# The orders, engine choices and buffer places of a five-engine kernel made anew

## The chip, the cores and the metric

The kernel runs on one core of a Trainium2 chip. A core has TensorE (PE, matrix products), VectorE (DVE), ScalarE (ACT), GpSimd (POOL) and SyncE (SP, which here issues every DMA); each works through its own queue of instructions in order, and a semaphore holds an instruction until what it needs is there. The metric is the device time of one execution in microseconds (us).

## The reference

Attention with random features, and then a feed-forward layer, on 8 batches of 8 heads with 576 rows of 64 elements:

```python
def phi(x):
    proj = np.einsum('bhsd,md->bhsm', x, omega)          # m = 128 features
    sq = np.sum(x * x, axis=-1, keepdims=True) / 2.0
    h = proj - sq
    h = h - np.max(h, axis=-1, keepdims=True)
    return np.exp(h) / np.sqrt(m)
q_p, k_p = phi(q * scale), phi(k * scale)
kv = np.einsum('bhsm,bhsd->bhmd', k_p, v)
z = np.sum(k_p, axis=2)
num = np.einsum('bhsm,bhmd->bhsd', q_p, kv)
den = np.einsum('bhsm,bhm->bhs', q_p, z)[..., None] + 1e-06
x = (num / den).transpose(0, 2, 1, 3).reshape(4608, 512)
h = x @ w_in                                             # 512 x 2048
out = np.maximum(0.01 * h, h) @ w_out                    # 2048 x 512
```

## The kernel before

The 4608 tokens are worked in 9 blocks of 512 (`NB`). For each block there are features of the queries (`query_block`), and for each batch features of the keys and the sums kv (`key_batch`); heads go in pairs `hp` of 0 to 3. Then `feed_forward` runs the block through both weights. Nearly every operand of the products is split into two float16 parts, a high one (a rounded copy, helper `high`, L689, L691 or L693) and a low one (the rest, helper `low_`, L699), and three matmuls take the place of one. The first two key batches and the first query block take an exact float32 way instead (class `Whole`, L1060 the projection, L1068 and L1076 its row maxima, L1078 the subtraction).

The weights have to be made ready in the opening. They come as 64-bit words in 8 pieces each (loads L810 and L812). A piece is put together from its bits on ACT, DVE and POOL (`Weight.convert`: L825 to L855), a column sum finds its scale (L845 on PE), and `Weight.split` makes the two parts (L691 or L693 the high one; L896 on DVE or L699 the low one). `values` finds the largest element of a batch's values (two reductions L1116 on DVE) and scales them (L1139). L733 with L737 to L742 turns a largest element into a power of two.

The names in the text: k*ij* and q*ij* are key batch or query block *i*, head pair *j*; w1*i* and w2*i* are the pieces of the two weights. L1189 and L1201 to L1203 are the sums kv, L1306 to L1308 (L1313 in block 0) the numerators, L1223 the low part of kv, L1283 and L1254 transposes by PE in block 0. L1468 and L1522 are the first layer (L1522 the seven-product form from block 2 on), L1704 the second one, L1629 the second one in the last two blocks. L783 is a warming matmul: it works on whatever lies in the omega tile and its result is not used.

What sets the order is `Plan`. Every step of the program becomes an `Op` with a number, the engines it can run on (`ways`) and the buffers it uses. `forward` is a list scheduler; here its order is thrown away, and `ORDER` gives the sequence in which all steps are written into the five queues, `ON` the engine of those that have a choice. The places of the buffers (which of the `row`, `big` or `ring` tiles a step gets) are still those that `forward` gave. The warming runs are placed by `forward` too (in gaps that it expects on PE before the first product of the feed-forward); `ORDER` names them by numbers past the last step.

```python
        if ORDER:
            by = {o.number: o for o in done}
            assert len(by) == len(ORDER)
            for n, e in ON.items():
                o = by[n]
                o.engine, (o.cost, o.run, o.held) = e, o.ways[e]
            done = [by[n] for n in ORDER]
```

## Time and profile before

| what | value |
|---|---|
| median of 3 runs | 909.47 us (908.52 to 910.31) |
| span of the profiled execution, first to last instruction | 907.4 us |
| median less span | 2.1 us |
| PE busy | 887.9 us, 98% |
| DVE busy | 790.7 us, 87% |
| ACT busy | 536.3 us, 59% |
| POOL busy | 240.5 us, 27% |

The span is what the trace shows from the first to the last instruction. The runs add about 2.1 us to it, the start and the end around the program. Busy time of PE counts the warming matmuls, and it counts a matmul from its start to its modelled end, so that a PE that is shown busy can still do nothing useful. Times in the trace are from the span's start.

### The profile page before, as it was taken

The numbers are of one execution on the slowest core, as the hardware profiler recorded it, in microseconds if no ns is written. First come the engines' busy times: TensorE is split into PE (matmuls) and PEld (weight loads), VectorE is DVE, ScalarE is ACT, GpSimd is POOL, SyncE is SP. The second block draws the span as 40 slices with busy tenths as digits, with TensorE's granted clock in tenths as the row PEclk, the third lists the DMA queues.
The fourth block names the chain that finished last, engine by engine and source line by source line (L and its number), as shares of the span: only waits on it lengthen the run. The fifth ranks groups of instructions, "written<-read, shape, count | busy, mean of one in ns | idle before, by whom it ended". The sixth has DMA issues, their size and how long they took to land.

```text
span 907.4 us, 20572 instructions
## 1 busy us (share of the span) xinstructions
PE 887.9 (98%) x8257; PEld 640.6 (71%) x8257; DVE 790.7 (87%) x1571; ACT 536.3 (59%) x825; POOL 240.5 (27%) x236
## 2 busy tenths in 40 slices
PE   7999989999999999999999999999999999999998
PEld 6888545554556975688568855886579656888887
DVE  7999989978999999999998999899998999952771
ACT  5688877467655774477546854686557533522530
POOL 2332234456341330220211330132001101331340
PEclk9999999999999999999999999999999999999999
DMA  9757456766899979897899897987999636443401
GB/s 353 282 212 220 123 122 139 181 179 138 180 225 230 270 209 208 231 251 178 195 231 225 196 257 167 245 232 157 187 201 252 156 78 215 146 101 115 164 1 47
DMA packets 274879, 170.13 MB, mean 187 GB/s; under 512 B 191072, under 2 KB 237920, under 8 KB 273760
## 3 DMA queue, kind: packets, MB, share of 16 engines
q1 hardware_dynamic: 274784, 168.82, 73.3%
q8 instruction: 64, 1.05, 0.5%
q14 instruction: 31, 0.25, 0.1%
HBM read 105.87 MB, written 16.78 MB: 135 GB/s over the span
## 4 chain that ended last, share of the span: by engine, by line
PE 75%; DVE 12%; DMA 6%; ACT 4%; issue 2%; SPq 1%; POOL 0%; ACTq 0%; DVEq 0%
PE late L1522 14%; PE late L1704 13%; PE ffn L1704 13%; PE ffn L1522 13%; PE pj L976 5%; PE late L1629 5%; PE ffn L1629 3%; PE late L1468 2%; PE ffn L1468 2%; DMA t<-qT 1%; PE mi L1306 1%; DMA nat<-kT 1%; DVE wt L835 1%; PE mi L1308 1%; PE mi L1307 1%
## 5 line engine op out<-in xcount | busy, mean ns | idle before, releaser
L1522 PEld LDWEIGHTS <-w 128*128 128x128 f16 x2352 | 228.0, 98 | 30.4 <-issue 0.5
L1704 PEld LDWEIGHTS <-big 128*128 128x128 f16 x1344 | 127.7, 98 | 138.2
L699 POOL TENSOR_TENSOR big<-row,big 128x512 f16<-128x512 f32 x76 | 92.5, 1222 | 307.1 <-ACT big L693 189.8
L1704 PE MATMUL late<-wt,big 128*128 128x512 f16 x672 | 157.5, 379 | 0.0
L1704 PE MATMUL ffn<-wt,big 128*128 128x512 f16 x672 | 157.0, 379 | 0.0
L1522 PE MATMUL late<-xt,w 128*128 128x256 f16 x864 | 117.9, 273 | 0.0
L1522 PE MATMUL ffn<-xt,w 128*128 128x256 f16 x840 | 114.9, 273 | 0.4 <-DMA xt<-v 0.4
L1007 ACT ACTIVATE p<-p,little 128x1024 f32<-128x1024 f32 (+1 forms) x60 | 61.0, 1016 | 63.0 <-DVE p L1004 52.9
L984 DVE TENSOR_REDUCE st<-pj 128x8 f32<-128x1024 f32 x68 | 73.2, 1077 | 10.6 <-PE pj L976 10.4
L699 DVE TENSOR_TENSOR ph<-p,ph 128x1024 f16<-128x1024 f32 x56 | 69.3, 1238 | 5.4 <-ACT ph L693 4.7
L1004 DVE SCALAR_TENSOR_TENSOR p<-pj,sc,st 128x1024 f32<-128x1024 f32 (+1 forms) x60 | 67.0, 1117 | 0.8
L1468 PEld LDWEIGHTS <-w 128*128 128x128 f16 x384 | 36.6, 98 | 40.3
L693 ACT ACTIVATE big<-row 128x512 f16<-128x512 f32 x92 | 56.3, 622 | 8.5 <-DVE row L1494 7.7
L1545 ACT ACTIVATE row<-row 128x512 f32<-128x512 f32 x71 | 43.7, 625 | 26.6 <-DVE row L1538 25.6
L936 ACT ACTIVATE z<-nat 128x512 f32<-128x512 f32 (+1 forms) x56 | 36.2, 646 | 31.8 <-DMA nat<-qn 16.2
L1522 PE MATMUL late<-w,w 128*128 128x256 f16 x324 | 53.0, 273 | 0.0
L1522 PE MATMUL ffn<-w,w 128*128 128x256 f16 x324 | 53.0, 273 | 0.0
L1468 PE MATMUL ffn<-xt,w 128*128 128x512 f16 x216 | 50.9, 379 | 0.0
L693 ACT ACTIVATE ph<-p 128x1024 f16<-128x1024 f32 x47 | 49.6, 1055 | 0.9
L699 POOL TENSOR_TENSOR v<-xp,v 128x1024 f16<-128x1024 f32 (+1 forms) x10 | 20.5, 2055 | 109.0 <-DVE v L689 49.4
L852 POOL TENSOR_TENSOR wt<-wt,wt 128x1024 f32<-128x1024 f32 x10 | 25.4, 2550 | 69.8 <-ACT wt L850 36.4
L938 DVE TENSOR_REDUCE sq<-z 128x8 f32<-128x512 f32 (+1 forms) x56 | 39.4, 705 | 4.1 <-ACT z L936 3.9
(300 smaller groups left out, 1893.3 us busy)
## 6 DMA issues: line engine op xcount, KB each, us to landing
w<-w1d SPq DMA_DIRECT2D x196, 256.0 KB, 3.8
v<-vn SPq DMA_DIRECT2D x28, 650.0 KB, 5.0
big<-w_in SPq DMA_DIRECT2D x8, 1024.0 KB, 10.3
big<-w_out SPq DMA_DIRECT2D x8, 1024.0 KB, 5.7
nat<-qn SPq DMA_DIRECT2D x32, 256.0 KB, 3.4
out<-row SPq DMA_DIRECT2D x31, 256.0 KB, 3.0
w1d<-wt SPq DMA_DIRECT2D x16, 256.0 KB, 3.4
nat<-kn SPq DMA_DIRECT2D x12, 320.0 KB, 4.7
```

The lines of the kernel that those rows point to most:

```text
L693: ("ACT", act(n, int(pointer)), lambda: nc.scalar.activation(dst(), src(), AF.Copy, scale=1.0 if scale is None else value()), False),
L699: return ways([(e, c, lambda g=g: g.tensor_tensor(dst(), a(), b(), op=ALU.subtract), True) for e, c, g in (("POOL", pool_(n), nc.gpsimd), ...
L938: op("DVE", dve(n), lambda: nc.vector.tensor_reduce(at(self.sq)[:, :2 * nt], square().rearrange("p (g d) -> p g d", d=D), axis=AX.X, op=AL ...
L976: nc.tensor.matmul(at(pj)[:, 512 * h + c * M:512 * h + (c + 1) * M], at(self.t)[:, 2 * (c0 + c) + h, :], om[:, w, :], start=(w == 0), stop ...
L984: op("DVE", dve(n * M), lambda: nc.vector.tensor_reduce(row(0), pv(), axis=AX.X, op=ALU.max), r=[pj], w=[st], prio=prio)
L1004: op("DVE", dve(n * M), lambda: nc.vector.scalar_tensor_tensor(p(), pv(), down(), row(2).rearrange("p (g o) -> p g o", o=1).broadcast_to([ ...
L1007: op("ACT", act(n * M, 1), lambda: nc.scalar.activation(flat(p()), flat(p()), AF.Exp, bias=shift), w=[p32], r=["ones"], prio=prio)
L1468: nc.tensor.matmul(at(ph), wk[wp][:, c:c + P], xt[:, 512 * xp:512 * xp + 512], start=(i == 0), stop=(i == 3 * KT - 1))
L1522: nc.tensor.matmul(pair(bank)[:, f], wt[:, k, wp, f * P:f * P + P], operand(xname, k, xp), start=(first and f == k == i == 0), stop=(k == ...
L1545: op("ACT", act(512), lambda: nc.scalar.activation(at(g), at(src), AF.Prelu, scale=H_DOWN * (TAIL_DOWN if tail else 1.0), alpha=0.01), r=[ ...
L1629: nc.tensor.matmul(pair(bank)[:, t], g()[:, gp, f, t * P:t * P + P], operand(wname, 2 * q + f, wp), start=(first and q == t == f == i == 0 ...
L1704: nc.tensor.matmul(at(po), g_(q)[:, s, gp, t * P:(t + 1) * P], wf[wp], start=(q == s == 0 and gp == wp), stop=(q == s == 3 and gp == 1))
```

## The change

No step of the program is added or taken away, and no dependency between steps changes. Three tables are new. `ORDER` has another sequence. `ON` gives other engines: between before and after, 28 of the 137 warming matmuls go, 25 low parts (L699) move from DVE to POOL, and DVE gets 9 steps net that ACT had (7 high parts or copies, 2 others). `PLACES` is new: it holds the buffer place of every buffer of every kind, in the order in which the buffers are made. A new function `settle` reads it and asserts that no place is handed out while it is in use. A negative number in `ORDER` stands for a run of so many warming matmuls; there are 9 such runs with 109 matmuls, where there were 10 with 137. `backward` and the passes that used it go; they did not run before (`PASSES = 0`).

```diff
-PASSES = 0
-SHIFT_OP = {...
...
+PLACES = {
+    "xt": [0, 1, 2, 3, 0, 1, 2, 3, 0, 5, 4, 1, 3, 2, 0, 1, 5, 3, 4, 1, 2, 0, 5, 1, 3, 2, 4, 0, 1, 3, 5, 2, 0],
+    "v": [0, 0, 0, 0, 0, 0, 0],
...
 ORDER = [
-    2, 16, 1, 0, 27, 62, 144, 151, 17, 7, 3, 43, 9, 4, 28, 165, 18, 5, 6, 146, 145, 22, 19, 152, 3478, 81, 3461, 20,
...
+    2, 0, 16, 1, 27, 43, 151, 3, 144, 7, 17, 4, 5, 22, 18, 28, 23, 6, 81, 44, 19, 62, 9, 24, 165, 20, -13, 33, 152,
...
-        done = self.forward()
-        for _ in range(PASSES):
...
-            done = [by[n] for n in ORDER]
+        if not ORDER:
+            return self.forward()
+        for o in self.ops:
+            o.engine, o.heat = ON.get(o.number, next(iter(o.ways))), False
+            o.cost, o.run, o.held = o.ways[o.engine]
+        done, heaters = [], len(self.ops)
+        for n in ORDER:
+            if n >= 0:
+                done.append(self.ops[n])
+                continue
+            x = Op()
+            x.number, x.engine, x.heat, x.filler, x.held = heaters, "PE", True, True, False
+            x.cost, x.run = -0.1 * n, lambda n=n: self.warm[1](-n)
+            x.ways, x.before, x.bufs = {"PE": (x.cost, x.run, False)}, [self.warm[0]], []
+            heaters += 1
+            done.append(x)
+        assert sorted(o.number for o in done if not o.heat) == list(range(len(self.ops)))
+        self.settle(done)
         return done
...
+                if b.place is None:
+                    b.place = PLACES[b.kind][nth[b]]
+                    assert b.place < self.places[b.kind]
+                    hosts = [(b.kind, b.place), *shared.get((b.kind, b.place), ())]
+                    assert not any(user.get(k) for k in hosts), f"{b.kind} {nth[b]} has a place in use"
+                    user[b.kind, b.place] = b
+                b.left -= 1
+                if not b.left:
+                    user[b.kind, b.place] = None
```

The lines of the kernel move by 48 (L699 is L747 in the changed one, L1116 is L1164, L1223 is L1271, L783 is L831, and so on). In the rows below a name with a number is a tile (`v_0_99` holds the values of batch 1, `pj_129` and `pj_0_133` are the banks of the projections, `mi` a bank of PE, `big` and `row` hold the hidden layer, `kv_100` the sums of batch 1).

On DVE, some 40 us into the program, where the maxima of the fourth key head pair of batch 0 and the value maxima of batch 1 stand. Before:

```order
53 L1116 TENSOR_REDUCE little<-v_0_99 128x1
54 L1068 TENSOR_REDUCE st_113<-pj_0_133 128x2
55 L1116 TENSOR_REDUCE little<-v_0_99 128x1
56 L1330 TENSOR_TENSOR xp_106<-mi_136,r_125 128x256
57 L833 TENSOR_SCALAR wt_72<-wt_70 128x1024
58 L835 SCALAR_TENSOR_TENSOR wt_72<-big_80,wt_72 128x1024
```

The changed kernel at the same place, and then where the value maxima stand now:

```order
54 L1374 TENSOR_SCALAR r_125<-mi_136,little 128x4
55 L1376 RECIPROCAL r_125<-r_125 128x4
56 L883 SCALAR_TENSOR_TENSOR wt_76<-big_82,wt_76 128x1024
57 L913 TENSOR_REDUCE little<-mi_136 128x8
58 L915 TENSOR_REDUCE little<-little 128x1
59 L1124 TENSOR_REDUCE st_112<-pj_129 128x8
```

```order
142 L998 TENSOR_SCALAR sc_121<-sc_121 128x1
143 L883 SCALAR_TENSOR_TENSOR wt_71<-big_79,wt_71 128x1024
144 L1164 TENSOR_REDUCE little<-v_0_99 128x1
145 L1032 TENSOR_REDUCE st_112<-pj_129 128x8
146 L747 TENSOR_TENSOR z_85<-nat_84,z_85 128x8x64
```

The two value maxima of batch 1 moved some 90 rows back, and the maximum of the projection in `pj_129` now stands in row 59, where it stood in row 64.

On DVE, just ahead of the numerators of q10 (they wait for the last part of batch 1's kv, `kv_100`). Before, and then the changed kernel:

```order
217 L994 SCALAR_TENSOR_TENSOR st_114<-st_114,sc_122,sq_118 128x8
218 L995 SCALAR_TENSOR_TENSOR st_114<-sq_118,st_114 128x8
219 L691 TENSOR_SCALAR kv_100<-mi_136 128x4
220 L1223 SCALAR_TENSOR_TENSOR kv_100<-mi_137,kv_100 128x4
221 L699 TENSOR_TENSOR big_80<-row_104,big_80 128x512
222 L1223 SCALAR_TENSOR_TENSOR kv_100<-mi_136,kv_100 128x4
```

```order
208 L1271 SCALAR_TENSOR_TENSOR kv_100<-mi_136,kv_100 128x4
209 L1042 SCALAR_TENSOR_TENSOR st_114<-st_114,sc_122,sq_118 128x8
210 L1043 SCALAR_TENSOR_TENSOR st_114<-sq_118,st_114 128x8
211 L739 TENSOR_SCALAR kv_100<-mi_137 128x4
212 L1271 SCALAR_TENSOR_TENSOR kv_100<-mi_137,kv_100 128x4
213 L747 TENSOR_TENSOR ph_90<-p_0_88,ph_90 128x1024
```

The last part of kv stood in row 222 of DVE's queue and stands in row 212; the low part of `ph_90`, ahead of it before, stands behind it.

On PE, where the projections of the third and fourth query head pairs of block 0 stand. Before, the run of 18 warming matmuls begins in the last two of these rows:

```order
273 L1060 MATMUL pj_129<-xt_108,nat_84 128x128 x2
274 L1060 MATMUL pj_129<-xt_108,p_0_88 128x128 x2
275 L1283 MATMUL ffn_135<-ident,ph_89 128x128 x4
276 L783 LDWEIGHTS om
277 L783 MATMUL mi_137<-om 128x240
```

```order
294 L1108 MATMUL pj_0_133<-xt_108,nat_83 128x128 x2
295 L1108 MATMUL pj_0_133<-xt_108,z_85 128x128 x2
296 L1361 MATMUL mi_137<-kv_100,qp_97 128x65 x4
297 L1108 MATMUL pj_129<-xt_108,xn_107 128x128 x2
298 L1108 MATMUL pj_129<-xt_108,p_0_88 128x128 x2
299 L1108 MATMUL pj_129<-xt_108,xn_107 128x128 x2
```

In the changed kernel the projections of both pairs follow the transposes at once, the fourth in the second bank; before, runs of 18, 5 and 27 warming matmuls stood ahead of the third.

## Rows read from the trace of the kernel before

**Rows 1.** Busy time of each engine in stretches of the opening; columns first.

```profile
core 0: us, PE busy (x) PEld busy (x) DVE busy (x) ACT busy (x) POOL busy (x), PEclk, DMA share, GB/s
23.00:46.00 23.00, 21.58 (x260) 19.99 (x259) 20.88 (x36) 15.30 (x23) 8.04 (x4) 1.00 0.71 283
0.00:73.50 73.50, 63.88 (x772) 58.80 (x773) 64.07 (x111) 53.44 (x74) 20.81 (x14) 1.00 0.76 287
0.00:138.30 138.30, 124.84 (x1209) 96.25 (x1210) 124.39 (x227) 104.01 (x151) 38.29 (x34) 1.00 0.65 215
```

**Rows 2.** The same view, from 139 us to the end.

```profile
139.00:300.00 161.00, 159.69 (x1277) 89.31 (x1271) 148.46 (x297) 102.95 (x149) 75.25 (x82) 1.00 0.80 189
300.00:500.00 200.00, 199.35 (x1991) 144.83 (x1989) 187.54 (x405) 123.41 (x194) 40.50 (x43) 1.00 0.91 221
500.00:780.00 280.00, 280.00 (x2645) 199.42 (x2643) 260.09 (x527) 165.74 (x260) 52.22 (x50) 1.00 0.83 194
780.00:903.40 123.40, 123.33 (x1129) 110.15 (x1126) 68.68 (x117) 39.51 (x73) 34.22 (x28) 1.00 0.31 92
```

**Rows 3.** Timeline of PE: start, length, instruction, idle time before it.

```profile
7.35 0.64 PE L1060 MATMUL pj<-xt,nat 64*128 64x128 f32 x4
7.78 0.64 PE L1060 MATMUL pj<-xt,z 64*128 64x128 f32 x4
9.44 0.39 PE L1060 MATMUL pj<-xt,nat 64*128 64x128 f32 x4
9.67 0.39 PE L1060 MATMUL pj<-xt,z 64*128 64x128 f32 x4
...
73.48 0.61 PE L1254 MATMUL ffn<-ident,xp 128*128 128x128 f32 x4
74.77 1.46 PE L1468 MATMUL ffn<-xt,w 128*128 128x512 f16 x6
...
124.39 1.05 PE L976 MATMUL pj<-om,t 128*128 128x128 f16 x16 [1.39 <-ACT p L1001]
138.29 0.19 PE L1307 MATMUL mi<-kv,qp 128*128 128x65 f16 x1 [0.26 <-DVE kv L1223]
```

**Rows 4.** Groups of instructions, PE: count, busy us, mean ns of one.

```profile
L783 PE MATMUL mi<-om 128*128 128x240 f16 x137 | 15.7, 266 | 0.6 <-DVE xp L1330 0.6
```

**Rows 5.** Timeline of DVE around the two marks.

```profile
45.25 1.22 DVE L1078 TENSOR_TENSOR ph<-pj,st 128x1024 f32<-128x1024 f32 x1
46.39 0.68 DVE L833 TENSOR_SCALAR wt<-wt 128x1024 uint32<-128x1024 uint32 x1
73.05 0.42 DVE L1330 TENSOR_TENSOR xp<-mi,r 128x256 f32<-128x256 f32 x1
128.71 3.38 DVE L896 SCALAR_TENSOR_TENSOR wt<-wt,little,wt 128x1024 f16<-128x1024 f32 x2
```

**Rows 6.** Groups of DVE's instructions in the first 139 us, by shape.

```profile
L1116 DVE TENSOR_REDUCE little<-v 128x1 f32<-128x1280 f32 x6 | 8.8, 1474 | 0.4 <-DMA v<-vn 0.4
L896 DVE SCALAR_TENSOR_TENSOR w<-wt,little,w 128x1024 f16<-128x1024 f32 x6 | 7.7, 1278 | 0.0
L1076 DVE TENSOR_REDUCE st<-pj 128x8 f32<-128x1024 f32 x11 | 13.4, 1217 | 0.8 <-PE pj L1060 0.8
L699 DVE TENSOR_TENSOR big<-row,big 128x512 f16<-128x512 f32 x5 | 3.3, 681 | 0.0
L691 DVE TENSOR_SCALAR w<-wt,little 128x1024 f16<-128x1024 f32 x1 | 0.8, 754 | 0.0
L689 DVE CAST big<-row 128x512 f16<-128x512 f32 x2 | 0.8, 419 | 0.0
L938 DVE TENSOR_REDUCE sq<-z 128x8 f32<-128x512 f32 x4 | 2.6, 677 | 0.0
```

**Rows 7.** Groups of POOL's instructions in the first 139 us, and one later piece's timeline.

```profile
L699 POOL TENSOR_TENSOR big<-row,big 128x512 f16<-128x512 f32 x8 | 9.3, 1183 | 25.7 <-ACT big L693 24.8 <-DMA t<-z 0.8
...
129.69 1.32 POOL L699 TENSOR_TENSOR big<-row,big 128x512 f16<-128x512 f32 x1 [8.97 <-ACT big L693]
```

More of the change, by code (lines that the diff above doesn't have):

```diff
@@ L282 @@
[L282 to L284 removed]
+    41: "DVE", 300: "DVE", 340: "DVE", 349: "DVE", 375: "DVE", 415: "DVE", 440: "DVE", 484: "DVE", 509: "DVE",
+    620: "DVE", 632: "DVE", 675: "DVE", 680: "DVE", 685: "DVE", 695: "DVE", 700: "DVE", 710: "DVE", 715: "DVE",
@@ L285 @@
+    3040: "DVE", 3052: "DVE", 3058: "DVE", 3070: "DVE", 3073: "DVE", 3165: "DVE", 3166: "DVE", 3180: "DVE",
+    3195: "DVE", 3203: "DVE", 3216: "DVE", 3223: "DVE", 3228: "DVE", 3237: "DVE", 3240: "DVE", 3244: "DVE",
+    3249: "DVE", 3255: "DVE", 3282: "DVE", 3309: "DVE", 3328: "DVE", 3351: "DVE", 3354: "DVE", 3363: "DVE",
+    3366: "DVE", 3375: "DVE", 3384: "DVE", 3394: "DVE", 3403: "DVE", 3415: "DVE",
 }
@@ L345, in order @@
     def order(self):
-        done = self.forward()
-        for _ in range(PASSES):
-            late = self.backward(done)
-            for o in self.ops:
-                if not o.filler and o.prio > -0.9:
-                    o.prio = -0.5 + 1e-4 * (late[o.number] + SHIFT_OP.get(o.number, 0.0))
-            done = self.forward()
-        if ORDER:
-            by = {o.number: o for o in done}
-            assert len(by) == len(ORDER)
-            for n, e in ON.items():
-                o = by[n]
-                o.engine, (o.cost, o.run, o.held) = e, o.ways[e]
-            done = [by[n] for n in ORDER]
@@ L361, in order @@
-        return done
-    def backward(self, done):
-        held, at_ = {}, {}
-        done = [o for o in done if not o.heat]
+        if not ORDER:
[14 more added lines that the diff above has]
+            done.append(x)
@@ new lines, in order, with settle @@
+        assert sorted(o.number for o in done if not o.heat) == list(range(len(self.ops)))
+        self.settle(done)
+        return done
+    def settle(self, done):
+        shared = {}
+        for k, hosts in self.over.items():
+            for h in hosts:
+                shared.setdefault(k, []).append(h)
+                shared.setdefault(h, []).append(k)
+        user, last, nth = {}, {}, {b: i for bs in self.kinds.values() for i, b in enumerate(bs)}
+        for bs in self.kinds.values():
+            for b in bs:
+                b.place, b.left = None, len(b.ops)
@@ L367, in backward @@
         for o in done:
-            o.needs = {x.number: x for x in o.before}
             for b in o.bufs:
-                if b not in at_:
-                    hosts = [(b.kind, b.place), *self.over.get((b.kind, b.place), ())]
-                    at_[b] = [held[k] for k in hosts if k in held]
-                    held[b.kind, b.place] = b
-                for x in (x for u in at_[b] for x in u.ops):
-                    o.needs[x.number] = x
-            o.needs.pop(o.number, None)
-        left = dict.fromkeys((o.number for o in done), 0)
@@ L378, in backward @@
-        for o in done:
-            for x in o.needs:
-                left[x] += 1
-        last = max(o.end for o in done)
-        until, late = dict.fromkeys(left, last), {}
-        free = dict.fromkeys(("PE", "ACT", "DVE", "POOL", "SP"), last)
-        port = last
-        todo = [o for o in done if not left[o.number]]
-        while todo:
-            cost = lambda o: o.cost - self.LESS[o.engine]
-            def latest(o):
-                r = min(until[o.number] - (o.end - o.start - cost(o)), free[o.engine])
-                return min(r, port) if o.held else r
-            o = max(todo, key=lambda o: (latest(o), o.start))
-            start = latest(o) - cost(o)
-            todo.remove(o)
-            late[o.number] = free[o.engine] = start
-            if o.held:
-                port = start
-            for n, x in o.needs.items():
-                until[n] = min(until[n], start)
-                left[n] -= 1
-                if not left[n]:
-                    todo.append(x)
@@ L403, in backward @@
-        return late
+                if b.place is None:
[7 more added lines that the diff above has]
+                    user[b.kind, b.place] = None
```

48 lines of the change are left out of this document (24 added, 24 removed), and 395 rows, old and new, of tables (ORDER, PLACES).

## The prediction

> **What bounds the kernel now.** I read first how busy each engine is by stretches. From 139 us on, PE is busy in 159.69 of 161 us, 199.35 of 200, 280.00 of 280 and 123.33 of 123.4 [rows 2]: 2.0 us of idle time in 764. Its matmuls follow each other there as fast as anywhere in the trace, so this stretch is PE's own work, and no order shortens it by more than those 2.0 us. What an order can change lies ahead of it. Up to 138.3 us PE is shown busy for 124.84 us, but 15.7 us of the whole trace are warming matmuls [rows 4], nearly all of them there, so PE does nothing useful in about 29 of these 138 us.
>
> What it waits for is DVE. DVE is busy 20.88 us of the 23 between 23 and 46 us, 64.07 of the first 73.5 and 124.39 of the first 138.3 [rows 1]. So between 73.5 and 138.3 us it is busy in 60.3 of 64.8 us. Two places show PE starting where DVE ends. Call them marks. **Mark 1** is the transposition L1254 for q02 at 73.48; the instruction that it needs, L1330, starts at 73.05 and takes 0.42 [rows 3, 5]. **Mark 2** is the numerator L1307 of q10 at 138.29, which waits for DVE's L1223 [rows 3]; behind it PE is full. As long as DVE is the engine that decides, a mark comes as early as the DVE work ahead of it is done, and what counts is that work less the useful PE work that is already behind PE.
>
> **The change, part by part.** At mark 1, the orders say what DVE has ahead of it. Gone are the two maxima of batch 1's values (2 x 1.474), and the high part (0.754) and low part (1.278) of w14, together 4.98 us; the high part goes to ACT and the rest stands later. In come a subtraction L1078 (1.22), a maximum L1076 (1.217), a low part of 1024 elements (near 1.25) and a short scaling (0.3), 3.99 us [rows 5, 6]. DVE is 1.0 us earlier. PE has more behind it there: the first product of the feed-forward (L1468, six matmuls, 1.3 us from 74.77 to the next) and the projection of k13, eight groups of four at 0.23 us from start to start (9.44 to 9.67), 1.8 us [rows 3]; the exchange of two numerators costs nothing. That is 3.1 us, and with DVE's 1.0 a gain of 4.1 us at mark 1.
>
> At mark 2 the difference is larger. Gone from DVE to ACT: two high parts of a weight piece (2 x 0.754), two of the hidden layer (2 x 0.419) and one of kv (about 0.42, from the same row), 2.77 us. Gone to POOL: four low parts of the hidden layer (4 x 0.681), 2.72 us. Moved behind the mark: a row sum of squares (0.677), the low part of a feature tile (1.22, the length of L1078, which has its shape) and the low part of a weight piece (1.278), 3.18 us. Come in: one low part (0.681) and one high part (0.419), 1.10 us [rows 5, 6]; a few instructions of under 0.3 us on either side are left out. The net is 7.6 us. DVE starts an instruction some 0.08 us before the one ahead has ended (45.25 + 1.22 against 46.39 [rows 5]), and eleven fewer of them give back 0.9, so 6.7 us. PE's own work at mark 2 is nearly the same, 0.5 us more behind it. The gain by DVE alone is 7.2 us.
>
> It isn't all realised. On the way from mark 1 to mark 2 PE also waits 1.39 us at 124.39 for ACT's L1001 [rows 3], which the change leaves alone, and DVE stands 4.5 us idle there for others. I take the 1.4 off: **5.8 us**, between the 4.1 of mark 1 and the 7.2 of mark 2, and the end of the program comes earlier by as much, since PE is full from mark 2 on.
>
> The rest is priced at nothing, with what covers it. The 28 warming matmuls fewer (28 x 15.7/137 = 3.2 us [rows 4]) lie in PE's waits, and give nothing of their own: without them PE would stand. They are how the shorter waits show. Five high parts more are ACT's in the opening, where it is busy 104.01 of 138.3 us [rows 1]; if ACT were late instead, 0.6 us each. The loads of batch 1's values go behind the weight's on SP's queue, and what is queued behind them is the feature and weight loads; they are needed only where DVE now takes their maxima, some 90 DVE rows later, which is the cover. After 139 us DVE is busy 148.46 of 161, 187.54 of 200 and 260.09 of 280 us [rows 2]; the other low parts go to POOL there, which makes room, and PE is the bound with or without it. The waits there, 2.0 us, are drawn anew by new places and orders: from -2.0 (all gone) to +4.0 (three times as many). I take 0.
>
> Warming is the one thing that could be missed. Early in the trace four projection matmuls are 0.43 us apart (7.35 to 7.78), and 0.23 from 9.0 us on (9.44 to 9.67) [rows 3]: the pace of 1.2 and of 2.4 GHz, though the granted clock is printed as 1.00 throughout [rows 1]. One more such slow stretch would cost the six groups of the first one 0.2 us each, 1.2 us; it is in the range.
>
> **Sum.** Span 907.4 - 5.8 = 901.6 us. The median of the runs is 2.1 us above the span: 903.7 us.
>
> **The rivals.** (1) *The gain is given back later.* PE gets to its full stretch earlier, but loads of the first layer's weights and the transposed rows must then come earlier too. In the new order the shortest stretch of PE work between the last use of a weight buffer and the next product from the same buffer is 36 matmuls, where it was 54. For it: the waits on DMA are already among those after 139 us. Against it: one buffer in 186, and 2.0 us in 764 is very little. With 6 us of waits instead of 2: 909.5 - 5.8 + 4.0 = 907.7 us.
>
> (2) *It does not do what it says*: the chain to mark 2 goes through loads, ACT and POOL as much as DVE, PE waits for the next of them, and nothing is won: 909.5 us. For it: DVE's 4.5 us idle between the marks are such waits. Against it: DVE busy for 93% of that time, and PE starting within 0.01 us of DVE's end at mark 1.
>
> (3) *Slower: POOL holds DVE up.* While a POOL low part runs, DVE's work from two buffers can stand: two L896 at 128.71 took 3.38 us, against 2 x 1.278, with a POOL low part from 129.69 to 131.01 in them [rows 5 to 7]. So a part that goes to POOL (1.183 us) may cost DVE more than it did on DVE (0.681). Ten such parts stand ahead of mark 2 in the new order, eight before. If each stopped DVE for its whole length, that is 11.8 us, less the 0.8 that is there already, against the 7.2 gained: 3.8 us later, 913.3 us. It decides from about 10 of the 11.8 us on. Against it: the eight of before cost only about 0.8 us of 9.3. The Trainium skill has this as a rule (SBUF — State Buffer, "Who interferes with whom"): the pair of ports that VectorE and GpSimd share is an exclusive lock for a whole instruction. By that rule in full the sum would be this rival's; the trace agrees at the one place above, and not in the other parts of the opening, so the chance is small.
>
> **How the numbers follow.** Forecast 0.68: gains from 4.1 us to 10.0 us (7.2, the 2.0 of later waits, and the 0.8 of the lengthened L896 pair), 899.5 to 905.4 us. Rival 1 0.15, spread from 906 to 909.4. Rival 2 0.10, around 909.5. Rival 3 0.07, above 911.3. 0.2%, about what a measurement of this kernel can tell from no change, is 1.8 us: faster means below 907.7, slower above 911.3. Faster is the forecast and half of rival 1, 0.75; same is the other half and rival 2, 0.18; slower 0.07. The range takes in the forecast and most of rival 1: 899.5 to 908.8 us.
>
> **What would show it.** In the changed trace, DVE's work ahead of q10's first numerators should be some 7 us less, and these should start at about 132 us; warming matmuls should take near 12.5 us, and no wait of PE for DVE should stand where runs of 18 and 27 stood; from there on PE should be full, with about 2 us idle. Wrong would be the forecast if PE's idle time after mark 2 grew to 6 us (rival 1), if mark 2 stood at 138 again behind waits for ACT or DMA (rival 2), or if DVE's parts from two buffers were longer by more than 9 us in sum (rival 3).

## The result: slower, by an opening that gained and a later part that lost

The changed kernel takes 913.56 us (median of 5 runs, 913.1 to 918.13) against 909.47: a ratio of 1.006 [1.0039, 1.0081]. The forecast was 903.7 us with a range of 899.5 to 908.8, so it is wrong in sign. Beside runs of before on two more chips, the same kernel took 923.36 us (1.0163 [1.0146, 1.0181]) and 919.37 us (1.0124 [1.0087, 1.0162]), while before stood at 908.3 and 908.1. Its three traces are called after, again and third below. The profiled execution of after is the slowest of its five, 918.13 us with a span of 916.4, so its trace holds 4.6 us more than the median. Times and ratios leave out one run below (935.3 us, without warming matmuls), which was in a slow state.

The stretches of after, in the columns of [rows 1] and [rows 2] (stretch, its length, busy us and count of PE, PEld, DVE, ACT and POOL, granted clock, DMA share, GB/s):

```profile
0.00:73.50 73.50, 68.22 (x829) 63.43 (x829) 66.06 (x123) 59.48 (x81) 21.75 (x19) 1.00 0.74 279
0.00:138.30 138.30, 133.01 (x1278) 100.31 (x1279) 129.58 (x235) 115.69 (x163) 46.34 (x41) 1.00 0.70 222
139.00:300.00 161.00, 156.48 (x1291) 92.12 (x1290) 140.72 (x289) 98.20 (x150) 83.21 (x83) 0.98 0.84 193
300.00:500.00 200.00, 193.54 (x1868) 138.02 (x1866) 180.81 (x385) 118.96 (x184) 49.28 (x49) 1.00 0.91 213
500.00:780.00 280.00, 272.90 (x2567) 191.56 (x2566) 242.23 (x498) 145.03 (x232) 64.82 (x59) 0.99 0.81 186
780.00:912.40 132.40, 132.35 (x1230) 118.47 (x1227) 81.56 (x150) 48.07 (x88) 36.53 (x30) 1.00 0.34 102
```

Two things have changed places. In the opening PE is busy for 133.01 us where it was 124.84 [rows 1], with fewer warming matmuls in it. From 139 us on, where before had 2.0 us of idle time [rows 2], the four stretches now leave 4.52, 6.46, 7.10 and 0.05: 18.1 us, and DVE is less busy too, 140.72 of 161 us against 148.46. So nobody is full there: the engines wait for each other. PE's waits in after from 139 us on (engine, operation and line <- engine, tile and line waited for: us in all, times, longest):

```profile
PE pj L1024 <- DVE p L1052: 7.8, 5, 3.7
PE late L1570 <- DMA w<-w1d: 5.1, 5, 2.2
PE mi L1354 <- DMA qp<-ph: 3.7, 1, 3.7
```

Lines of the changed kernel are 48 higher than before's: L1024 is before's L976 (the product behind a pair's features), L1570 its L1522, L1354 its L1306. They wait for DVE, for weights and for transposed rows: several causes. But the places are the same ones. Counting PE's products from the start, without the warming matmuls, nine waits stand ahead of the same products in all three traces: the 1219th, 2235th, 3047th, 3341st, 3699th, 4305th, 5613th, 6355th and 6449th. They are 16.1 of after's 18.1 us, and 14.1 of 15.7 and 13.8 of 16.0 in the other two.

**A measure for the rest.** Idle time misses what PE loses at a lower clock or between matmuls. So I took, for every shape and line of matmul, the median distance from its start to the next start between 139 and 900 us, and added these up over all matmuls but the warming ones. The time passed less that sum is PE's *lost time* up to a point; the end is PE's last matmul. It can be held against the spans: at the end it is 20.9 us for before and 29.9 for after, 9.0 apart as the spans are (916.4 and 907.4). Only differences between rows are to be read. The float32 projections of the opening start by turns some 7 and 105 ns after the one ahead, a median does not fit them, and for it all rows are about 20 us too low, so that after's 2.6 us by 139 us is less than its idle time.

| lost by (us) | 139 | 300 | 500 | end | from 139 on |
|---|---|---|---|---|---|
| before | 15.8 | 18.2 | 19.8 | 20.9 | 5.1 |
| after | 2.6 | 10.7 | 19.4 | 29.9 | 27.3 |
| again | 10.0 | 17.1 | 23.3 | 33.6 | 23.6 |
| third | 9.5 | 15.9 | 24.2 | 32.1 | 22.6 |

By 139 us the changed kernel is 13.2, 5.8 and 6.3 us ahead. Behind that it loses 22.2, 18.5 and 17.5 us more than before.

**Two of the places** that all three traces share. The first, around 275 us in after (start, length, instruction; idle time before it in brackets):

```profile
273.80 2.13 POOL L747 TENSOR_TENSOR v<-xp,v 128x1024 f16<-128x1024 f32 x1 [5.24 <-ACT v L741]
273.81 2.15 DVE L1042 SCALAR_TENSOR_TENSOR st<-st,sc,sq 128x8 f32<-128x8 f32 x1
...
277.49 1.28 DVE L1052 SCALAR_TENSOR_TENSOR p<-pj,sc,st 128x1024 f32<-128x1024 f32 x1
...
278.82 1.87 PE L1024 MATMUL pj<-om,t 128*128 128x128 f16 x16 [3.72 <-DVE p L1052]
```

A DVE step of 128x8 that takes 0.22 us elsewhere takes 2.15, about as long as POOL's low part beside it; 1.5 us of small steps stand between it and L1052; and PE waits 3.72 us. The same place costs 4.24 us in again and 3.43 in third. Behind the wait PE runs at half clock (stretches of after):

```profile
274.00:278.00 4.00, 1.10 (x11) 0.83 (x9) 3.86 (x9) 1.19 (x2) 1.93 (x1) 0.96 1.01 331
278.00:284.00 6.00, 5.18 (x55) 4.67 (x55) 3.19 (x4) 3.69 (x6) 0.00 (x0) 0.50 0.99 283
```

The second is SP's queue and PE at 626 to 636 us in after:

```profile
626.00 3.25 SPq L1291 DMA_TRANSPOSE xt<-xn  x1
629.35 3.67 SPq L1291 DMA_TRANSPOSE w<-v  x1
633.07 1.31 SPq L1322 DMA_TRANSPOSE qp<-ph  x1
...
636.25 0.24 PE L1354 MATMUL mi<-kv,qp 128*128 128x65 f16 x1 [3.70 <-DMA qp<-ph]
```

The transpose that PE needs could have gone from 608.86 us on, when ACT had made its source, and stood behind two large ones that held SP for 6.9 us. PE waits 3.70.

### The profile page after: what moved, and what is told of

The parts are those of the page before. It is cut to its first block, busy times and chain, and to the rows that moved or that the text cites. A ratio compares the mean times of both kernels' runs of the same rounds, so it can differ in the third digit from the quotient of the medians.

```text
span 916.4 us, 20491 instructions
## 1 busy us (share of the span) xinstructions
PE 889.0 (97%) x8229; PEld 640.8 (70%) x8229; DVE 776.5 (85%) x1555; ACT 526.2 (57%) x816; POOL 280.9 (31%) x261
## 4 chain that ended last, share of the span: by engine, by line
PE 47%; DVE 6%; DMA 3%; SPq 2%; issue 1%; ACT 1%; POOL 0%; DVEq 0%; POOLq 0%; ACTq 0%
PE late L1570 10%; PE ffn L1752 8%; PE ffn L1570 8%; PE late L1752 8%; PE ffn L1677 5%; PE late L1677 3%; PE pj L1024 3%; DMA w<-w1d 1%; DMA nat<-kn 1%; DVE ph L747 1%; SPq L1291 1%; DVE st L1032 1%; DVE p L1052 1%; PE mi L1354 1%; DVE z L1009 1%
## 5 line engine op out<-in xcount | busy, mean ns | idle before, releaser
L1570 PEld LDWEIGHTS <-w 128*128 128x128 f16 x2352 | 227.9, 98 | 41.3 <-DMA w<-w1d 6.3
L747 POOL TENSOR_TENSOR big<-row,big 128x512 f16<-128x512 f32 x87 | 108.1, 1249 | 277.9 <-ACT big L741 139.1
L1570 PE MATMUL late<-xt,w 128*128 128x256 f16 x942 | 129.5, 274 | 0.7 <-DMA w<-w1d 0.4
L1570 PE MATMUL ffn<-xt,w 128*128 128x256 f16 x762 | 105.1, 273 | 0.0
L747 DVE TENSOR_TENSOR ph<-p,ph 128x1024 f16<-128x1024 f32 x56 | 69.9, 1248 | 2.4 <-ACT ph L741 2.3
L1052 DVE SCALAR_TENSOR_TENSOR p<-pj,sc,st 128x1024 f32<-128x1024 f32 (+1 forms) x60 | 67.0, 1117 | 0.6
L1570 PE MATMUL late<-w,w 128*128 128x256 f16 x342 | 56.0, 273 | 4.7 <-DMA w<-w1d 4.7
L984 ACT ACTIVATE z<-nat 128x512 f32<-128x512 f32 (+1 forms) x56 | 36.0, 644 | 30.6 <-DMA nat<-kn 10.4
L747 POOL TENSOR_TENSOR xn<-xp,xn 128x768 f16<-128x768 f32 (+2 forms) x13 | 23.7, 1824 | 93.9 <-DVE xn L737 44.2
L1570 PE MATMUL ffn<-w,w 128*128 128x256 f16 x306 | 50.1, 273 | 0.8 <-DVE z L1586 0.7
L1516 PE MATMUL ffn<-xt,w 128*128 128x512 f16 x204 | 48.3, 379 | 0.0
L1024 PE MATMUL pj<-om,t 128*128 128x128 f16 x576 | 40.7, 224 | 5.3 <-DVE p L1052 5.3
```

What stands on the lines that cost most here:

```text
L747: return ways([(e, c, lambda g=g: g.tensor_tensor(dst(), a(), b(), op=ALU.subtract), True) for e, c, g in (("POOL", pool_(n), nc.gpsimd), ...
L1024: nc.tensor.matmul(at(pj)[:, 512 * h + c * M:512 * h + (c + 1) * M], at(self.t)[:, 2 * (c0 + c) + h, :], om[:, w, :], start=(w == 0), stop ...
L1052: op("DVE", dve(n * M), lambda: nc.vector.scalar_tensor_tensor(p(), pv(), down(), row(2).rearrange("p (g o) -> p g o", o=1).broadcast_to([ ...
L1516: nc.tensor.matmul(at(ph), wk[wp][:, c:c + P], xt[:, 512 * xp:512 * xp + 512], start=(i == 0), stop=(i == 3 * KT - 1))
L1570: nc.tensor.matmul(pair(bank)[:, f], wt[:, k, wp, f * P:f * P + P], operand(xname, k, xp), start=(first and f == k == i == 0), stop=(k == ...
```

## Experiments: where the loss lies

Two theories first: the changed sequence behind the opening is itself the slower one; or PE, being ahead, cannot keep a lead that the others can't follow, and any sequence would give it back. So the two kernels were cut and joined: the changed one's opening to 200 us with before's sequence and engines from there, the reverse, and a cut at 575 us. The buffer places were given out anew in these joined kernels, longest free first. In the list of step numbers, the beginning of the first against before's, and its seam (629 is the last step in the changed kernel's sequence):

```diff
 ORDER = [
-    2, 16, 1, 0, 27, 62, 144,
+    2, 0, 16, 1, 27, 43, 151,
...
     699, 711, 689, 920, 854, 629, 921, 690, 572, 1197, 1189, 855,
...
```

> The changed kernel's order and engines for every step that it has begun by 200 us of its trace, and then the order and engines of the kernel before from its 213 us on (the two have done the same steps there, but for 3.5 us of DVE work and 4 us of POOL work; the places of the buffers of the second part are given out again, the one longest free first). At 200 us the changed kernel is 12.2 us ahead of the kernel before in PE's work, and it gives back 21 us from there to the end in the profiled execution. Theory 1 (the waits after the opening belong to the places of the new sequence): the second part keeps the 5 us of lost time that it had, and the lead stays: 909.5 - 12.2 = 897.3 us, 896 to 900. Theory 2 (the lead cannot be held, since DVE, busy 90 to 94% between 139 and 430 us, is the next bound and takes it back whatever the sequence): the lead melts in new waits of PE for DVE before 430 us, 906 to 910 us.

> The opposite graft: the kernel before up to its 213 us, then the changed kernel's order and engines from its 200 us on. Theory 1 (the sequence): the changed kernel's second part loses its 17 to 21 us here too (17 by the median of its runs, 21 by its profiled execution): 926 to 931 us, with the stalls before L1024, L1570 and L1354 in the same places of the program. Theory 2 (the lead): PE comes 12 us later and DVE with it is no more behind than it was in the kernel before; the waits that ate the lead (275 to 430 us, some 11 us) are gone and only those after 630 us stay (9 us): 916 to 919 us.

> The changed kernel up to its 575 us, then the order and engines of the kernel before from its 576.5 us on, places given out again. At 575 us the changed kernel's lead is down to 0.3 us; the 9.2 us that it falls behind come between 630 and 725 us, where PE waits for the transposed queries (L1354, 3.9 us), for weights (L1570, 3 to 4 us) and for little else. Theory 1 (the sequence): these 9 us go and nothing else changes, 904.5 (median less 9) to 909 us (kernel before less 0.3). If they are a matter of what the first 575 us left behind (buffers, queues), they stay: 912 to 915 us.

> The changed kernel once more, for a second trace. Theory 1 and 2: the stalls of PE come at the same steps as in the first trace (before L1024 at 275, 428 and 497 us, before L1354 at 632 us, before L1570 at 394 and 716 us); what varies is their length, and whether PE's clock falls after those of over 3 us. 913 to 918 us. If the stalls sit elsewhere, the trace of one execution says little on where the time goes.

| kernel | us | ratio | lost by 139 | 300 | 500 | end | from 139 on |
|---|---|---|---|---|---|---|---|
| changed to 200, then before | 903.8 | 0.9951 [0.9936, 0.9965] | 9.5 | 12.3 | 14.5 | 15.6 | 6.1 |
| before to 200, then changed | 934.03 | 1.0271 [1.0248, 1.0295] | 15.4 | 24.4 | 32.0 | 46.0 | 30.6 |
| changed to 575, then before | 921.02 | 1.0149 [1.0122, 1.0175] | 9.8 | 14.1 | 20.9 | 31.1 | 21.3 |

None of these four runs took the time that a theory gave it. The first joined kernel lies between its two forecasts: its opening lost 9.5 us by 139 us, as again's did, so the lead was 6.3 us and not 12.2. The other two are slower than either theory said, and again took 923.36 us where 913 to 918 was expected, with its waits at the expected steps.

The first settles it all the same. It comes to 139 us 6.3 us ahead of before and ends 5.3 ahead, 4.5 us in the medians (908.33 to 903.8). Its stretches after 139 us are before's again ([rows 2]):

```profile
139.00:300.00 161.00, 159.29 (x1307) 92.01 (x1306) 146.71 (x298) 106.35 (x161) 80.12 (x83) 1.00 0.85 199
300.00:500.00 200.00, 199.14 (x1978) 144.21 (x1976) 188.15 (x399) 124.66 (x193) 40.06 (x42) 1.00 0.93 218
500.00:780.00 280.00, 280.00 (x2637) 198.97 (x2635) 260.15 (x529) 162.60 (x257) 52.03 (x50) 1.00 0.83 196
```

The lead can be kept, and the second kernel, without a lead, loses 30.6 us behind the opening, a part of it at its seam (waits of 1.38 and 2.43 us at 219 and 226): the theory of the lead falls. The loss belongs to the changed sequence behind some 200 us, with its engines. Nor does it need the buffer places of the changed kernel: in the second 821 of 1681 places are others, and six of the nine waits stand ahead of the same products in it (2235, 3341, 3699, 5613, 6355 and 6449). The cut at 575 us says little on what lies behind it, since the seam itself costs most: 21.8 us are lost by 550 and 30.2 by 600.

**Single places.** The next theory: a handful of badly placed steps make the loss. Two kernels mend the named places by moving steps within one queue, one on DVE and one on SP (seven buffer places with it); one puts warming matmuls ahead of the two products that waited, against the lower clock.

```diff
-    1006, 1240, 1241, 1302, 1303, 1141, 1242,
+    1240, 1241, 1242, 1006, 1302, 1303, 1141,
...
-    2239, 2714, 2386,
+    2239, 2714, 2473, 2386,
...
-    1243, 1262,
+    1243, -32, 1262,
```

The first pair, in which steps of the other engines are left out, puts L1052 (1242) ahead of the small steps of another head pair and of a division (1006); two more L1052 and L1009 are moved alike. The second puts q63's transpose (2473) ahead of the large ones; two weight loads are moved alike. The third is the first of two warming runs.

> The changed kernel beside the three runs that follow, which mend it in places. 913 to 923 us: on the chip of its first runs it was 913.6, on the next one 923.4; the difference stood at 125 us already (2.7 against 10.0 us of PE's time lost by then), where low parts on POOL had come 0.1 us ahead of a step of DVE instead of behind it.

> The changed kernel with three steps of DVE put first where PE waits for them, nothing else: the subtraction L1052 of q30 ahead of four small steps and of the division L1403 that lets POOL start a low part (PE waited 3.7 and 4.2 us there, at 279 and 287 us, DVE's step L1042 had taken 2.15 us beside that low part where it takes 0.22); L1052 of q43 ahead of L1009 (which took 2.12 for 0.74 us beside POOL; PE waited 1.7 us at 430); L1052 of q52 ahead of the five steps L785 to L790 (PE waited 0.8 us at 498). Theory 1 (the waits belong to single places of the sequence): all three go, and with the first the fall of PE's clock: 7 to 9 us less than the changed kernel. Rival (PE is ahead of DVE all over, a wait that is taken away comes back at the next step): under 3 us less.

> The changed kernel with three issues of SP put first: the transposes of q63 (ready 25 us earlier, they stood behind two transposes L1291 that took 3.3 and 3.7 us of SP; PE waited 3.7 and 2.5 us at 636 and 641) ahead of those two; one weight load ahead of the two transposes L1291 at 709 us, and one ahead of a transpose at 386 us (PE waited 2.2 and 1.2 us at 719 and 722, 1.8 and 1.2 us at 396 and 401). Theory 1: these three waits go, with the fall of the clock behind the first: 6 to 9 us less than the changed kernel. Rival (SP's queue is full, something else stands back in its place): under 3 us less, with new waits for transposes or weights within 20 us of the old ones.

> The changed kernel with 32 warming matmuls (3.2 us) ahead of the step that PE waits for at 279 us and 22 (2.2 us) ahead of that at 636 us. They fill waits and remove none: what they can give back is what PE's lower clock costs behind the two waits (granted clock 0.5 of full from 278 to 284 us and from 636 to 639.6 us in the first trace). Theory 1 puts 1.1 to 2.5 us on the first fall and 1.3 to 1.5 us on the second (time lost there less the wait itself): 2.5 to 4 us less than the changed kernel. If the falls cost nothing that counts: the same time within 1 us, or more where a warming run is longer than the wait that is left.

Beside third's 919.37 us they took 918.61, 919.43 and 922.56, with 29.5, 31.0 and 33.7 us lost at the end against 32.1. The first two came out as their rivals said; the third is slower, where a gain or no change was expected. Each mended wait goes or shrinks, and others come. PE's waits from 139 us on with DVE's steps moved:

```profile
PE mi L1342 <- DMA qp<-ph: 2.5, 1, 2.5
PE late L1558 <- DMA w<-w1d: 2.0, 3, 1.0
PE pj L1012 <- DVE p L1040: 1.9, 3, 0.7
PE late L1558 <- ACT row L729: 1.7, 1, 1.7
PE late L1558 <- DVE row L725: 1.2, 1, 1.2
PE late L1558 <- DMA xt<-v: 1.2, 1, 1.2
```

and with SP's steps moved (lines here are 12 lower than after's):

```profile
PE pj L1012 <- DVE p L1040: 7.2, 5, 2.6
PE ffn L1558 <- DVE row L1574: 2.8, 1, 2.8
PE late L1740 <- DVE nat L1574: 2.4, 1, 2.4
```

In the first, waits for L1040 (after's L1052) fall from 7.8 to 1.9 us. The product mended first, the 2235th, starts at 281.61 without a wait, and 4 to 12 us further on, from 285 to 293, the 2281st, 2308th and 2329th wait 1.66, 1.19 and 1.21 us for ACT, for a transposed row and for DVE. In the second the wait of 3.70 us for transposed rows is gone, and waits of 2.75 and 2.44 us stand at 400 and 729, ahead of the 3329th product (12 before a mended one) and of the 6543rd (94 behind another). Warming does keep the clock up at both places (its stretches):

```profile
280.00:284.00 4.00, 3.73 (x41) 3.42 (x39) 3.38 (x9) 0.39 (x1) 0.68 (x1) 1.00 1.07 330
636.00:640.00 4.00, 3.30 (x47) 2.74 (x45) 1.99 (x8) 1.46 (x3) 0.00 (x0) 1.00 0.35 66
```

yet it is the slowest of the three: by 725 us it has lost some 2 us more than third. A wait of 2.73 us for weights stands at 721 us, where third's is 1.47; what holds the weights up there isn't shown. So the theory of single places falls in this form: the waits have their places, but when one is mended the next stands within 100 products of it. The six mended places hold the longest waits, and with all six mended (below, on another chip) 4.4 us of the loss are gone, a quarter.

**Engines or sequence.** Is it the choice of engines (`ON`) or the sequence? Each was tried with the other's partner; 249 steps differ in engine: net, 25 go from DVE to POOL and 8 from ACT to DVE.

> The changed kernel's sequence and places with the engines of the kernel before: 249 steps change their engine (44 of DVE's go to POOL by the change and 19 of POOL's to DVE, 97 of ACT's to DVE and 89 of DVE's to ACT; here they all go back). Theory E (the engines: low parts on POOL stand in DVE's way, 21 us of lengthened steps of DVE after 139 us against 14 before): the waits for DVE go, 905 to 912 us. Theory S (the sequence: PE, DVE and SP are each needed by the next one with no time between, whoever does a step): no better than the changed kernel, 915 to 930 us, since DVE gets 14 us of work back.

> The opposite: the kernel before, sequence and places, with the changed kernel's engines. Theory E: the low parts that go to POOL lengthen DVE's steps here too and PE waits for them: 914 to 925 us. Theory S: the kernel before's sequence holds, 907 to 912 us, within 3 us of the kernel before.

The changed sequence on before's engines takes 950.14 us (1.0457), before's sequence on the changed engines 948.05 (1.0443), with 63.4 and 58.9 us lost. Both are 24 us and more worse than either whole kernel, and beyond what either theory gave. This says that sequence and engines are one thing, each made for the other, and tells nothing on which of them is the weak one in the changed kernel.

**POOL's low parts.** The changed kernel has 25 more of them on POOL. In two kernels POOL's writes zeros in their place, so that it reads nothing from SBUF; a third does so with all six places mended, and a fourth mends these alone.

```diff
-        return ways([(e, c, lambda g=g: g.tensor_tensor(dst(), a(), b(), op=ALU.subtract), True)
+        runs = {"POOL": lambda: nc.gpsimd.memset(dst(), 0.0),
+                "DVE": lambda: nc.vector.tensor_tensor(dst(), a(), b(), op=ALU.subtract)}
...
```

> The changed kernel with every low part that POOL works out (L747 on POOL, 145 of them) set to zero by POOL instead, so that it reads nothing and is done sooner: what it leaves out is that subtraction, and the output lacks those parts. Theory L (what the new sequence cannot bear is that POOL's two-operand steps hold DVE up): most of the 21 us of lengthened DVE steps go, and with them the waits of PE for L1052 and the loss at 105 to 125 us; 12 us or more off the changed kernel: 895 to 910 us. Theory F (no time to spare anywhere, POOL is one of several): 3 to 8 us off, waits for weights and for turned queries stay: 911 to 918 us.

> The kernel before with the same left out (119 low parts on POOL set to zero). Its sequence hides the 14 us of lengthened DVE steps that it has after 139 us (PE waits 2 us there), so only the opening can gain, where DVE is the bound and lost 1 us to POOL. Theory L and F: 905 to 909.5 us. If it gains more than 5 us, POOL holds up the opening in a way that the durations of DVE's steps do not show.

> The changed kernel with POOL's low parts set to zero (as in n_after_low0: that subtraction is left out) and the six steps of m1 and m2 put first. n_after_low0 took 910.1 us; its PE still waits 2.2 us at 278, 1.0 at 391, 2.0 at 629 and 2.4 at 709 us, all at places that are mended here, with some 3 us of lower clock behind them. If these waits belong to their places once DVE is not held up: 902 to 905 us, under the kernel before. If a mended wait comes back in another place in this case too: 907 to 912 us.

> The changed kernel with the six steps of m1 and m2 put first and its low parts as they are. m1 and m2 each came out within 1 us of the changed kernel on their chip (919.4), 2.5 and 1 us less by their traces. If their gains add up: 914 to 919 us. If the waits go round: 918 to 923 us.

| kernel | us | ratio | lost by 139 | from 139 on |
|---|---|---|---|---|
| changed, POOL writes zeros | 910.09 | 1.0009 [0.9996, 1.0021] | 3.7 | 18.0 |
| before, POOL writes zeros | 908.55 | 0.9996 [0.9981, 1.0011] | 14.1 | 6.1 |
| changed, six places, zeros | 907.68 | 0.9989 [0.9977, 1.0001] | 3.2 | 15.3 |
| changed, six places | 917.26 | 1.0087 [1.0063, 1.0111] | 10.6 | 18.2 |

The first time lies between the ranges of theories L and F. With six places mended, the kernel with zeros lies in the range given for waits that come back elsewhere, the one without them in that for gains that add up. For before the zeros are worth nothing. For the changed kernel they are worth some 10 us: 9.6 between the last two rows, which ran on one chip. Of the lost time, 7.4 us of that lie in the opening and 2.9 behind it (without the six places, against third on another chip, 5.8 and 4.6). One caution: the write takes 541 ns against 1249 for a low part of the same shape, so the edit frees POOL's own time as well. The largest group of POOL's writes in the first of the four kernels (line, engine, operation, count | busy us, mean ns | idle before it):

```profile
L747 POOL MEMSET big<- 128x512 f16 x99 | 50.5, 541 | 75.7 <-PE late L1754 44.1 <-PE ffn L1754 21.5 <-PE ffn L1679 10.2
```

How it costs 7 us in the opening is seen where after and again part. After at 95 us:

```profile
95.38 2.43 POOL L747 TENSOR_TENSOR big<-row,big 128x512 f16<-128x512 f32 x1 [2.07 <-ACT big L741]
...
95.57 1.22 DVE L903 SCALAR_TENSOR_TENSOR wt<-wt,wt 128x1024 uint32<-128x1024 uint32 x1
```

and again, at 96 us:

```profile
96.46 1.29 POOL L747 TENSOR_TENSOR big<-row,big 128x512 f16<-128x512 f32 x1 [2.07 <-ACT big L741]
...
96.65 2.18 DVE L903 SCALAR_TENSOR_TENSOR wt<-wt,wt 128x1024 uint32<-128x1024 uint32 x1
```

The same two steps, 0.19 us apart in both, and only one of them at full speed: in after POOL's is stretched from 1.29 to 2.43 us, in again DVE's from 1.22 to 2.18. In again more DVE steps behind it are held (L1042 takes 1.15 us, L883 2.10, L881 1.14, L1271 1.84), PE waits 2.71 us up to 119.03, and the granted clock is 0.50 from 119 to 122 us. The Trainium skill has this (SBUF — State Buffer, "Who interferes with whom"): the port pair that VectorE and GpSimd share is an exclusive lock, and whoever issues first has it for its whole instruction. The traces agree that one of the two stands. Which one was first they do not show: eleven traces have these two steps in this order, POOL's starts 0.16 to 0.21 us ahead of DVE's in every one, and DVE stands in nine, POOL in two (after and the kernel without warming matmuls below). So after's opening is the lucky one, and the expectation for third, which puts it down to 0.1 us ahead or behind, does not hold.

Could the opening be freed of it by order alone? In the joined kernel three DVE steps were moved: a maximum L1164 of batch 1's values (418) ahead of L903 (260), a row maximum of q11 (495) later and a low part of kv (42) earlier. The first of them:

```diff
-    260, 322, 418,
+    418, 260, 322,
...
```

> The graft of the changed kernel's first 200 us on the kernel before's rest, once more on another chip, and beside the next one: 903 to 904 us where the head loses 10 us of PE by 139 us as in its first run, down to 897 where it loses 2.6 as in the changed kernel's first trace.

> That graft with three steps of DVE moved between 96 and 116 us, so that a step that POOL's low parts did not lengthen in any trace (a reduction, L1164 or L1032) stands where a low part runs: the reduction of v1 ahead of L903 of w25, the reduction L1032 of q11 behind the column sums L923, the small L1271 of k01 ahead of a reduction. In the graft's first trace low parts on POOL lengthened L903, L1042, L883 and L1271 there by 0.97, 0.93, 0.88 and 1.7 us, and PE waited 2.7 us at 118 us and lost 2 more at its lower clock. Theory: 3 to 5 us less than the graft (DVE is what the opening waits for). If POOL's next low part falls on the step that moves up, as chance has it: the same within 1.5 us.

The joined kernel took 904.64 us again (0.995 [0.9933, 0.9967]), and with the steps moved 902.95 (0.9933 [0.9913, 0.9952]), lost by 139 us 10.6 and 10.2. The held step is now another one (timeline of the second, DVE, beside a POOL step of 3.28 us from 111.79):

```profile
112.79 2.31 DVE L1027 SCALAR_TENSOR_TENSOR st<-st,sc,sq 128x8 f32<-128x8 f32 x1
115.14 1.07 DVE L1028 SCALAR_TENSOR_TENSOR st<-st,sq 128x8 f32<-128x8 f32 x1
```

The gain of 1.7 us lies between the two forecasts, and the intervals overlap, so the move isn't shown to help; either is faster than both kernels compared here.

**Is there reserve in before?** What remained: perhaps before's sequence takes a small delay without harm, and the changed one doesn't. In before, one row maximum of q30 was made three times, some 2.5 us more on DVE in the full stretch; and the changed kernel was run without its warming matmuls.

```diff
+                for _ in range(3 if (self.what, self.i, self.hp) == ("q", 3, 0) else 1):
+                    nc.vector.tensor_reduce(row(0), pv(), axis=AX.X, op=ALU.max)
...
-    -13, 33, 152,
+    33, 152,
```

> The kernel before with one reduction of DVE (L984 of q30, at 287 us) run three times instead of once: 2.2 us more of DVE at the place where the changed kernel's DVE was held up by 1.9 us and PE lost 5 to 6.5 us. The result is the same. Theory F (a full PE has no time to spare, in this sequence either): PE waits about 2 us there and falls to its lower clock if it waits over 3; 2 to 5 us more than the kernel before: 910.5 to 913.5 us. Rival (the kernel before's sequence has time to spare there): within 1 us of the kernel before.

> The changed kernel without its 109 warming matmuls, all else the same. The prediction took 28 fewer for nothing, since DVE is what the opening waits for: if that holds for all of them, within 2 us of the changed kernel. Rival: without them PE's clock stays low in stretches of the opening, in which PE then comes later than DVE: 3 to 8 us more, seen as a granted clock under 1.00 between 12 and 73 us.

Before with the late step takes 912.19 us, 1.0034 [1.0022, 1.0046]: 2.8 us for 2.5 on DVE, as theory F said. DVE's step and PE's wait in that kernel, and then the wait of before at the same place:

```profile
287.54 3.73 DVE L986 TENSOR_REDUCE st<-pj 128x8 f32<-128x1024 f32 x3
```

```profile
PE mi L1205 <- DVE ph L699: 2.8, 1, 2.8
...
PE mi L1203 <- DVE ph L699: 0.3, 1, 0.3
```

All of the delay reaches PE, a few us later, and little is won back; but nothing follows from it either (lost time is 2.7 us above before's by 300 us and 2.1 at the end, and the granted clock stays at 1.00 around the wait). So at this one place, where PE waits for DVE in before too, before has no reserve: PE is full because the steps ahead of it are just in time. The diff shows the first of the nine warming runs that were taken out. Without them the runs of the changed kernel spread from 920.3 to 932.7 us (1.019 [1.0126, 1.0255] against before), and parts of the opening have a mean granted clock between the two levels:

```profile
12.00:20.00 8.00, 5.06 (x50) 4.87 (x52) 5.71 (x8) 5.15 (x7) 0.33 (x1) 0.71 0.85 347
```

Its profiled execution, the fastest, has lost 7.4 us by 139 us, where after, in which the same step of POOL stands at the start, has lost 2.6: that speaks for the rival, at some 5 us between two traces on two chips. The unaltered changed kernel did not run on that chip, so what the warming matmuls are worth in the end isn't shown.

## Why the prediction was wrong

**The opening** was forecast by the right engine. Numerators of q10 were to start at about 132 us; they start at 125.19 in after and at 132.55 in again; in before they start at 137.84. The gain by 139 us was to be 5.8; it was 13.2, 5.8 and 6.3. The stretches up to these numerators in before, after and again (columns of [rows 1]):

```profile
0.00:137.84 137.84, 124.64 (x1208) 96.14 (x1209) 123.93 (x225) 103.73 (x150) 38.29 (x34) 1.00 0.65 216
...
0.00:125.19 125.19, 119.91 (x1180) 93.39 (x1180) 116.89 (x217) 102.89 (x146) 40.09 (x35) 1.00 0.67 227
...
0.00:132.55 132.55, 122.93 (x1180) 94.26 (x1180) 122.71 (x217) 103.15 (x146) 38.86 (x35) 0.99 0.62 214
```

DVE's work is 7.0 us less in after (123.93 to 116.89), just as forecast. Two terms were missed. DVE's idle time falls as well, from 13.9 us to 8.3 and 9.8, where I took 1.4 us off the gain for waits. And in again the same 217 steps take 5.8 us longer than in after, beside POOL's low parts. That the gain came out at 5.8 and 6.3 in two traces is luck: the two nearly cancel. The second is rival 3's mechanism, which I had held to cost what it did in before, some 0.8 us [rows 5, 7].

**The warming matmuls** that are gone cost nothing in themselves: the opening's clock is 1.00 in after, and the slow pace of the first projections ends at 8.07 us, where it was about 9 [rows 3]. Nothing can be said from this of the other 109, without which the opening ran at a lower clock.

**The step that failed** is "The waits there, 2.0 us, are drawn anew by new places and orders: from -2.0 (all gone) to +4.0 (three times as many). I take 0", and with it that the end comes earlier by as much as mark 2, "since PE is full from mark 2 on". Measured, lost time behind 139 us grew by 22.2, 18.5 and 17.5 us, and idle time from 2.0 to 18.1, 15.7 and 16.0. The ground for it was that PE is the bound there "with or without it", the room that POOL makes. A full PE [rows 2] was read as if the others had time in hand; the late step shows that at one place they had none, and crossing sequence and engines, 40 us either way, shows how far it can go wrong. Since `ORDER`, `ON` and `PLACES` were all new behind the opening, the range should have been that of an order not yet seen: 2.0 us downwards, and tens upwards.

**Rival 1** named a right cause with a wrong size: weights that come late are 5.1 us of after's 18.1 and 2.8 of again's 15.7, less than a third; waits for DVE's features are 7.8 and 8.2.

**What the loss consists of.** From third's 17.5 us of growth, the six places give 4.4 (22.6 to 18.2) and POOL's locks with them another 2.9 (18.2 to 15.3); these are differences between single traces, the first one between two chips, so the sizes are rough. Some 10 us (15.3 less before's 5.1) are left. In the kernel with both mended PE still stands for 10.2 us from 139 us on, mostly for DVE; its longest waits (lines are 10 to 12 lower than after's):

```profile
PE late L1742 <- DVE nat L1576: 2.9, 1, 2.9
PE ffn L1560 <- DVE row L1576: 1.7, 3, 0.8
PE late L1560 <- ACT row L729: 1.6, 1, 1.6
PE late L1560 <- DVE row L725: 1.0, 1, 1.0
```

These too have their places: ahead of the 2281st, 2329th, 3329th and 6543rd product, near the mended ones, where the mended kernels without zeros have them as well. They come with the sequence behind 200 us and its engines, and not with the opening or the lead; other buffer places do not remove the loss, and warming against the lower clock at two places won nothing. What in the sequence makes them stays open, and whether the changed places add to the loss was not tried by itself.

## What to carry to other kernels

An engine that is full says that nobody is late, not by how little: before trusting it against a new order, count what is just in time, or delay one step and see whether it arrives. When an order made by hand or by a planner changes everywhere, forecast the untouched-looking stretches as widely as the ones it was made for, and try the good part alone: here the opening by itself, with before's tail, is worth 4.5 and 3.7 us on two chips, and the whole loses 4 to 15. Compare waits by the product they stand ahead of, and not by time: what looks scattered in three traces turned out to be nine places.

## What the chip showed that I had not expected

- POOL's low parts hold even the smallest DVE steps: 128x8 in 2.15 us for 0.22. Which engine stands can differ between runs in which the recorded starts are alike (nine traces against two above). The changed kernel took 913.6, 919.4 and 923.4 us on three chips, where before stayed between 908.1 and 909.5; that the locks are all of this spread isn't shown.
- A POOL step that only writes can still hold one of DVE's. In before with zeros, a cast that has 0.69 us elsewhere takes 3.65 beside writes on POOL from 263.21 to 266.49 (DVE's timeline). The section of the Trainium skill named above says so of casts, and that steps with two inputs stand only for a POOL step that reads:

```profile
263.39 3.65 DVE L689 CAST ph<-p 128x1024 f16<-128x1024 f32 x1
```

- Ten of the 32 large transposes L1291 in after keep SP for 3.1 to 5.4 us, where the shortest take 1.2. Some let go about when the last DMA issued before them lands: one at 710.87 us in after took 4.68 us, with that landing 4.62 behind its start; one in before at 462.98 took 5.60, and 5.81. But one at 709.23 in after took 1.60 with such a landing 4.95 behind, so what decides isn't shown. What stands behind them on SP waits as long.
